# A gated linear-attention block with a SiLU-gated layer behind it: where the weights and activations begin in SBUF

## The chip, the cores and the metric

The kernel runs on one core of a Trainium2 chip. What counts is the device time of one execution in microseconds; the median of three runs is given. Each core has a matrix engine (PE in the profile, with its weight loads as PEld), a vector engine (DVE), a scalar engine (ACT), GpSimd (POOL), and a queue engine (SP) that starts the DMA transfers. SBUF is the on-chip memory of 128 partitions, PSUM the memory into which the matrix engine accumulates.

## What is computed

Per batch and head a complex 48 x 48 state is decayed step by step and read out by `q`; the result `x` (3072 tokens x 384) goes through a SiLU-gated layer. Cut to what matters:

```python
mag = np.sqrt(a_re * a_re + a_im * a_im)
scale = np.minimum(mag, 0.999) / (mag + 1e-06)
a_re_n, a_im_n = a_re * scale, a_im * scale
for t in range(S):                                   # S = 768, D = 48, 4 batches, 8 heads
    new_re = ar * S_re - ai * S_im
    new_im = ar * S_im + ai * S_re
    S_re, S_im = new_re + outer(k[t], v[t]), new_im
    y[t] = q[t] @ S_re
x = y.transpose(0, 2, 1, 3).reshape(3072, 384)
g = x @ w_gate                                       # 384 x 1536
out = (g / (1 + np.exp(-g)) * (x @ w_val)) @ w_out   # 1536 x 384
```

The weights arrive as 64-bit numbers; the kernel turns them into 32-bit ones on the chip.

## The kernel before

The tokens are cut into 24 slabs of 128 (6 chunks of time by 4 batches). Two slabs make a group, so there are 12 groups `g` of 256 tokens. The 1536 hidden columns of the gated layer are cut into 12 chunks `f` of 128. For each group the recurrence is turned into matmuls: `stage_ops` makes the decay factors on ACT and DVE, `slab_ops` the scores (line 630), the readout (line 661) and the state's update (line 667), and running sums over time are matmuls with a triangle of ones (line 457; line 454 in the first groups). The readout ends as `xh`, the group's activations rounded to the matrix engine's 32-bit fast format, and `xl`, the remainder.

`ffn_ops(g)` then runs over the 12 chunks. For each chunk, `f1` (line 847) makes gate and value: for each of the two, and for each of three slices of the 384 inputs, the products high weight x `xh`, high weight x `xl`, low weight x `xh`. That is 18 matmuls of 256 columns. In them a 128 x 128 block of weights is the stationary operand, and the activations are the moving operand, read as 256 consecutive 4-byte words of each partition. ACT applies SiLU (853), DVE multiplies with the value (858), and the product is split in the same way into `hh` and `hl` (lines 311, 313 and 307). `f2` (line 881) multiplies with `w_out`: two halves of 128 tokens by three products, 6 matmuls of 384 columns. Here the roles are turned: `hh` or `hl` is stationary, and the weights are moving, 384 consecutive words. Group 0 is exact: it uses the whole weights in single products in plain 32-bit, 6 in `f1` and 4 records per chunk in `f2`, reading every second word of the 64-bit storage.

The order of all instructions is made when the program is written, by a planner (`Planner.plan`) that holds an estimated cost for each step and hands out a fixed list. It knows costs, dependences, the number of buffers and due times (`key`), and nothing of addresses. The matrix engine works through its list in order; so does each other engine.

Where the operands lie. `place(nm, f, dtype)` (line 221) makes a tile of a chunk's weights: 1536 words of a partition for gate and value (`nm` "w"), 768 for `w_out` ("o"). The 64-bit words of chunk `f` are loaded into `place(nm, f)` by SP (line 737), put together on DVE (lines 746, 750, 754), and split into high and low halves (`c4`, `c5`) into the tile of the chunk before, `place(nm, f - 1)`. From then on chunk `f` is read from there: the high half at the tile's start, the low half 768 or 384 words behind it. Before the weights come, some of these tiles are lent to group 0's stages (`fixed`, line 268); after the split, the last chunk's tiles (`spare`, line 227) take the transfers for the range checks (line 795) and sector checks (818). `new(tag, inst)` (line 279) makes the other tiles. For the tags in `SHIFTED` (`xh`, `xl`, `hh`, `hl`) it makes the tile 64 words longer and begins 48 words, three times 64 bytes, behind its start.

Of the kernel before, what the change touches and what calls it, by code (L numbers as in the profile page):

```python
# [19 lines left out]
P = 128  # L20
# [172 lines left out]
def quick(ctx, tc, q, k, v, a_re, a_im, w_gate, w_val, w_out, out, count):  # L193
# [4 lines left out]
    work = ctx.enter_context(tc.tile_pool(name="work", bufs=1))  # L198
# [20 lines left out]
    WIDE = {"w": 2 * DM, "o": DM}  # L219

    def place(nm, f, dtype):

        return work.tile([P, 2 * WIDE[nm]], dtype, name=f"w{nm}{f}", tag=f"w{nm}{f}", bufs=1)

    tile_t = const.tile([P, 4 * DM], F32, name="turned")

    def spare(nm):

        if nm not in W:
            W.pop((nm, NF - 1, WHOLE))  # L230
            W[nm] = place(nm, NF - 1, F32)
        return W[nm]
# [21 lines left out]
    for t in STAGES:  # L254
        SHAPE[t] = ([P, 2 * H, D], F32)
    slots = dict(qs=1, ks=1, T=2, dec=3, sc=2, sg=2, hh=2, hl=2, ost=2, xh=2, xl=2, vt=2,
                 gv=2, po=1, ps=2, py=1, pm=1)
# [6 lines left out]
    for t, (nm, f, i) in {"re": ("w", 0, 0), "im": ("w", 0, 1), "s1": ("o", 0, 0), "s2": ("w", 1, 0), "s3": ("w", 1, 1),  # L264
                          "qt": ("o", 1, 0), "kt": ("o", 2, 0), "qs": ("w", 2, 0)}.items():
        n, nm_f = 96 if t == "qs" else D, (nm, NF - 3 + f)
        if nm_f not in W:
            W[nm_f] = place(*nm_f, F32)
        at = W[nm_f][:, i * A2:i * A2 + 2 * H * n].rearrange("p (h d) -> p h d", d=n)
        for j in range(2):  # L270
            fixed["lent", t, j] = at[:, H * j:H * j + H], nm_f
# [4 lines left out]
    pl = Planner(slots)  # L276
    at_ = {}

    def new(tag, inst):
        if tag in fixed:  # L280
            t = fixed[tag][0]
        elif tag[0] in ("ww", "wo", "bt"):
            t = None
        elif tag in PSUMS:
            t = psum.tile([P, 512], F32, name="p_" + tag, tag=tag, bufs=2 if tag == "po" else slots[tag])
        else:
            shape, dt = SHAPE[tag]
            if isinstance(inst, tuple) and inst[0] in SPLIT:
                dt = F32R
            if tag == "xh" and inst == 0:  # L290
                dt = F32
            if tag == "xl" and isinstance(inst, str):
                dt = U32
            if tag in SHIFTED:
                n = shape[-1] * (shape[1] if len(shape) > 2 else 1)
                t = work.tile([P, n + 64], dt, name=tag, tag=tag, bufs=slots[tag])[:, 48:48 + n]
                if len(shape) > 2:
                    t = t.rearrange("p (k t) -> p k t", k=KT)
            elif tag == "dec":
                t = work.tile([96, 8 * H], dt, name=tag, tag=tag, bufs=slots[tag])[:, 0:4 * H]  # L300
            else:
                t = work.tile(shape, dt, name=tag, tag=tag, bufs=slots[tag])
        at_[tag, inst] = t
        return t
# [26 lines left out]
    def stage_ops(g, first, many):  # L331
# [19 lines left out]
        def load(t, x):  # L351
            def fn(e):
                b0 = 2 * bp + first
                nc.sync.dma_start(out=new(*tg(t)).rearrange("p (b h) d -> p b (h d)", b=many), in_=x[b0:b0 + many, :, c * P:c * P + P, :].rearrange("b h t d -> t b (h d)"))
            pl.add(f"ld_{t}{N}", {"SP": 0.5}, fn, deps=[held.get(t, "")], alloc=[tg(t)], lat=1.4 if N == "0a" and t in ("re", "im") else LAND if exact else LAND + SPARE, move=0.65 * many)

        def act(name, dst, source, func, table, deps, scale=1.0, bias=None, new_=False):
            def fn(e):
                if new_:
                    new(*tg(dst))  # L360
                kw = {} if bias is None else {"bias": bias}
                nc.scalar.activation(out=of(dst), in_=of(source), func=func, scale=scale, **kw)  # L362
            length = cost(("ACT",), span)
            if bias is not None:
                length["ACT"] += 0.1
            pl.add(name + N, length, fn, deps=[d if "." in d else d + N for d in deps] + [held.get(name, "")], alloc=[tg(dst)] if new_ else [],
                   use=[tg(source)] + ([] if new_ else [tg(dst)]), table=table)
# [4 lines left out]
        if divided:  # L372
            def rec(e):
                nc.vector.reciprocal(out=new(*tg("s3")), in_=of("re"))
            pl.add("rec" + N, {"DVE": 2.5 * span / HD}, rec, deps=["ld_re" + N], alloc=[tg("s3")], use=[tg("re")])
        else:
            act("lnr", "s3", "re", AF.Ln, "ln", ["ld_re"], new_=True)
# [343 lines left out]
    def weight_ops(f):  # L721
        for nm, n, user in (("w", 2 * DM, "f1"), ("o", DM, "f2")):
# [5 lines left out]
            for i, w in enumerate((w_out,) if nm == "o" else (w_gate, w_val)):  # L728
                def ld(e, i=i, w=w, raw=raw, nm=nm):
                    if i == 0:  # L730
                        W.pop((nm, f), None)
                        W[nm, f, WHOLE] = place(nm, f, U32)
                        raw["all"] = W[nm, f, WHOLE].rearrange("p (n t) -> p n t", t=2)
                        raw["low"], raw["high"] = (raw["all"][:, :, x] for x in range(2))
                    o = raw["all"]
                    o = o if nm == "o" else o[:, i * DM:i * DM + DM].rearrange("p (k n) t -> p k n t", k=KT)
                    nc.sync.dma_start(out=o, in_=words(w, nm, f))
                loads.append(pl.add(f"wl{i}{N}", {"SP": 0.55}, ld, alloc=[] if i else lent, deps=list(loads), lat=LAND, move=1.09))
# [360 lines left out]
@with_exitstack  # L1099
def tile_kernel(ctx, tc, q, k, v, a_re, a_im, w_gate, w_val, w_out, out):  # L1100
    nc = tc.nc
    w_gate, w_val, w_out = (w if w.dtype == U32 else w.bitcast(U32) for w in (w_gate, w_val, w_out))
    keep = ctx.enter_context(tc.tile_pool(name="keep", bufs=1))

    count = keep.tile([1, 32], I32, name="count")[:, 0:1]
    quick(tc, q, k, v, a_re, a_im, w_gate, w_val, w_out, out, count)
    fit = nc.values_load(count, min_val=0, max_val=P)
    with tc.If(fit < P):
        general(tc, q, k, v, a_re, a_im, w_gate, w_val, w_out, out)
# [34 lines left out]
```

## Time and profile before

| what | value |
|---|---|
| median of 3 runs | 634.52 us (634.34 to 634.69) |
| the profiled execution's own time | 634.72 us |
| its span, first to last instruction | 632.9 us |
| PE busy | 615.9 us (97%) |
| DVE busy | 492.1 us (78%) |
| ACT busy | 427.0 us (67%) |
| POOL busy | 37.7 us (6%) |
| granted clock of PE, mean | 0.997 |
| moved by DMA | 80.66 MB, mean 127 GB/s |

The span leaves 1.8 us of the execution's time outside. Busy times of PE overlap and their ends are modelled, so a matmul's cost is read from the start of one to the start of the next, not from its duration. The chain of work that ended last says which engine sets the end; the timeline and the windows show the pace inside a stretch.

### The profile page before, as it was taken

Reading aid. Unit: us, or ns where it says so; the run is one execution under the profiler, and the core shown is the slowest. Engines: PE = TensorE matmul, PEld = TensorE weight load, DVE = VectorE, ACT = ScalarE, POOL = GpSimd, SP = SyncE. Lnnn points to the kernel's source line nnn. Section 1 sums busy time; section 2 is a strip of 40 time slices with the busy share of each in tenths; the row PEclk is TensorE's granted clock in tenths of the full one; section 3 lists DMA queues with packets and bytes.
Section 4 is the critical chain, followed back from the end, with each engine's and each line's share of the span. In section 5 each row is a group of like instructions: output and inputs, shape, how many; then the busy total and the mean of one; then the engine's idle time right before and its main releaser. Section 6 shows DMA issues by size and latency. Waiting matters only on the chain.

```text
span 632.9 us, 15752 instructions
## 1 busy us (share of the span) xinstructions
PE 615.9 (97%) x6380; PEld 590.9 (93%) x6380; DVE 492.1 (78%) x896; ACT 427.0 (67%) x693; POOL 37.7 (6%) x64
## 2 busy tenths in 40 slices
PE   8889999999999999999999999999999999999995
PEld 7677788899999999999999999999999999999995
DVE  6999999999978888779758779768769767543432
ACT  7973677987856976967967867977968973212210
POOL 1310001001010001001000010010000000000000
PEclk9999999999999999999999999999999999999998
DMA  9999213344463554464444464454443433421200
GB/s 284 324 337 305 38 50 94 74 111 123 121 149 108 147 135 117 122 150 116 129 123 119 122 163 110 118 152 127 127 125 104 139 85 94 122 74 51 76 1 30
DMA packets 133983, 80.66 MB, mean 127 GB/s; under 512 B 94320, under 2 KB 130160, under 8 KB 133904
## 3 DMA queue, kind: packets, MB, share of 16 engines
q1 hardware_dynamic: 131648, 75.52, 43.7%
q0 software_dynamic: 2256, 4.06, 2.9%
q8 instruction: 52, 0.85, 0.6%
q14 instruction: 27, 0.22, 0.1%
HBM read 59.04 MB, written 4.78 MB: 101 GB/s over the span
## 4 chain that ended last, share of the span: by engine, by line
PE 72%; DVE 3%; ACT 3%; issue 1%; ACTq 0%; DVEq 0%
PE p_gv L847 38%; PE p_po L881 20%; PE p_py L661 6%; PE p_ps L630 5%; PE p_pm L457 2%; PE p_pm L667 2%; ACT L971 1%; ACT s L362 1%; DVE wo L307 0%; DVE ww L307 0%; DVE sg L858 0%; DVE s L307 0%; DVE hl L307 0%; DVE sc L636 0%; ACT sg L853 0%
## 5 line engine op out<-in xcount | busy, mean ns | idle before, releaser
L847 PE MATMUL p_gv<-xh,ww 128*128 128x256 f32 x1596 | 310.1, 291 | 2.3 <-DVE sg L858 1.4
L847 PEld LDWEIGHTS p_gv<-xh,ww 128*128 128x128 f32 x1596 | 258.2, 190 | 9.1 <-DVE sg L858 3.2
L847 PE MATMUL p_gv<-xl,ww 128*128 128x256 f32 x726 | 203.0, 280 | 0.0
L971 ACT ACT_TABLE_LOAD x123 | 157.8, 1283 | 2.2
L847 PEld LDWEIGHTS p_gv<-xl,ww 128*128 128x128 f32 x726 | 136.4, 188 | 0.0
L853 ACT ACTIVATE sg<-p_gv 128x256 f32<-128x256 f32 x144 | 54.7, 383 | 106.6 <-PE p_gv L847 102.4
L881 PE MATMUL p_po<-wo,hh 128*128 128x384 f32 x484 | 126.4, 342 | 0.0
L858 DVE TENSOR_TENSOR sg<-sg,p_gv 128x256 f32<-128x256 f32 x144 | 59.0, 412 | 67.4 <-ACT sg L853 66.9
L881 PEld LDWEIGHTS p_po<-wo,hh 128*128 128x128 f32 x484 | 80.8, 188 | 1.1 <-issue 0.2
L881 PE MATMUL p_po<-wo,hl 128*128 128x384 f32 x242 | 81.5, 337 | 0.0
L307 DVE TENSOR_TENSOR hl<-sg,hh 128x256 fp32r<-128x256 f32 x132 | 55.0, 418 | 5.8 <-ACT hh L311 1.5
L630 PE MATMUL p_ps<-T 96*128 96x128 f32 x384 | 52.9, 279 | 0.0
L630 PEld LDWEIGHTS p_ps<-T 96*128 96x128 f32 x384 | 50.9, 196 | 0.6
L311 ACT CAST hh<-sg 128x256 fp32r<-128x256 f32 x68 | 27.5, 404 | 33.1 <-PE p_po L881 15.3
L881 PEld LDWEIGHTS p_po<-wo,hl 128*128 128x128 f32 x242 | 45.4, 188 | 0.0
L362 ACT ACTIVATE s<-s 128x768 f32<-128x768 f32 x44 | 37.2, 845 | 9.5 <-DVE s L307 7.6
L661 PE MATMUL p_py<-sc,vt 128*32 128x128 f32 x768 | 36.5, 272 | 1.1 <-ACT xh L685 1.1
L661 PE MATMUL p_py<-T,G 96*32 96x128 f32 x640 | 33.5, 280 | 0.0
L636 DVE TENSOR_TENSOR sc<-p_ps,tri 128x512 f32<-128x512 f32 x48 | 32.4, 678 | 0.5 <-PE p_ps L630 0.3
L847 PE MATMUL p_gv<-xh,ww-1_399 128*128 128x256 f32 x132 | 25.3, 283 | 0.0
L685 ACT CAST xh<-p_py 128x384 fp32r<-128x384 f32 x22 | 10.5, 478 | 21.6 <-PE p_py L661 21.4
L661 PEld LDWEIGHTS p_py<-sc,vt 128*32 128x32 f32 x768 | 22.8, 109 | 2.4 <-ACT xh L685 1.3
(140 smaller groups left out, 856.9 us busy)
## 6 DMA issues: line engine op xcount, KB each, us to landing
T<-turned SPq DMA_DIRECT2D x240, 64.0 KB, 2.1
wo<-in_moe_w_out_dram SPq DMA_DIRECT2D x24, 384.0 KB, 5.5
ww<-in_moe_w_gate_dram SPq DMA_DIRECT2D x12, 384.0 KB, 8.0
vt<-in_v_dram SPq DMA_DIRECT2D x24, 192.0 KB, 3.9
ww<-in_moe_w_val_dram SPq DMA_DIRECT2D x12, 384.0 KB, 8.6
out_dram<-ost SPq DMA_DIRECT2D x24, 192.0 KB, 2.0
wo<-in_moe_w_gate_dram SPq DMA_DIRECT2D x12, 384.0 KB, 3.6
wo<-in_moe_w_val_dram SPq DMA_DIRECT2D x12, 384.0 KB, 3.5
```

What stands on the lines that cost most here:

```text
L307: V[e].tensor_tensor(out=out, in0=a, in1=b, op=op)
L311: nc.scalar.copy(out=out, in_=in_)
L362: nc.scalar.activation(out=of(dst), in_=of(source), func=func, scale=scale, **kw)
L457: nc.tensor.matmul(out=ps, lhsT=tri, rhs=flat(half(x, i)), start=j == 0, stop=j == 1)
L630: nc.tensor.matmul(out=ps[:, hh, :], lhsT=kT(4 * qd + hh), rhs=qT(4 * qd + hh), start=True, stop=True)
L636: nc.vector.tensor_tensor(out=s, in0=at_["ps", f"{n}.{qd}"].rearrange("p (h t) -> p h t", h=4), in1=mask.unsqueeze(1).to_broadcast([P, 4, ...
L661: nc.tensor.matmul(out=o, lhsT=l, rhs=r, start=opens, stop=closes, tile_position=(0, 32 * slot))
L847: nc.tensor.matmul(out=gv[:, i, :], lhsT=l, rhs=r, start=(m == 0), stop=(m == len(mm) - 1))
L853: nc.scalar.activation(out=new("sg", I), in_=at_["gv", I][:, 0:2 * P], func=AF.Silu)
L858: nc.vector.tensor_tensor(out=sg, in0=sg, in1=at_["gv", I][:, 2 * P:4 * P], op=ALU.mult)
L881: nc.tensor.matmul(out=po, lhsT=l[:, cs], rhs=weight("o", f, part), start=f == 0 and j == 0, stop=f == NF - 1 and j == len(products) - 1)
L971: nc.scalar.preload_act_table_set(op.load)
```

## The change

Each tile of weights grows by 16 words (64 bytes). Its content begins `2 * ((f + 1) % 8)` words behind the tile's start, with `f` the number of the tile. Chunk `f` of the split weights lies in tile `f - 1`, so it begins `2 * (f % 8)` words, 0 to 56 bytes, behind a multiple of 64 bytes: chunks 0 and 8 at 0, chunks 1 and 9 at 2 words, and so on up to chunk 7 at 14 words. The loads of the raw words into tile `f` and the work lent to these tiles begin at that tile's offset too. For the tags of `SHIFTED` the content begins 48 words behind the tile's start in even groups, as before, and 50 words in odd groups. As a matmul's blocks are 128, 256 or 384 words apart, all operands of a chunk or group share its offset. No step is added, taken away or reordered. Tiles that are allocated behind a tile of weights move by whole multiples of 64 bytes.

```diff
     def place(nm, f, dtype):
 
-        return work.tile([P, 2 * WIDE[nm]], dtype, name=f"w{nm}{f}", tag=f"w{nm}{f}", bufs=1)
+        n, at = 2 * WIDE[nm], 2 * ((f + 1) % 8)
+        return work.tile([P, n + 16], dtype, name=f"w{nm}{f}", tag=f"w{nm}{f}", bufs=1)[:, at:at + n]
...
+    def tag_group(inst):
+
+        if isinstance(inst, int):
+            return inst
+        return int(inst.split(".")[0]) if "." in inst else 0
...
             if tag in SHIFTED:
                 n = shape[-1] * (shape[1] if len(shape) > 2 else 1)
-                t = work.tile([P, n + 64], dt, name=tag, tag=tag, bufs=slots[tag])[:, 48:48 + n]
+                begin = 48 + 2 * (tag_group(inst) % 2)
+                t = work.tile([P, n + 64], dt, name=tag, tag=tag, bufs=slots[tag])[:, begin:begin + n]
```

## Rows read from the trace of the kernel before

**Rows 1.** The page: busy time and share of each engine, and the chain that ended last by engine and by line.

```profile
PE 615.9 (97%) x6380; PEld 590.9 (93%) x6380; DVE 492.1 (78%) x896; ACT 427.0 (67%) x693; POOL 37.7 (6%) x64
...
PE 72%; DVE 3%; ACT 3%; issue 1%; ACTq 0%; DVEq 0%
```

**Rows 2.** Busy time of each engine in stretches of the span, with the granted clock of PE, the DMA engines' share and what they moved.

```profile
20.00:40.00 20.00, 16.11 (x248) 13.71 (x247) 19.85 (x34) 17.26 (x31) 6.16 (x9) 1.00 1.09 330
40.00:60.00 20.00, 18.27 (x91) 14.92 (x92) 20.00 (x36) 10.55 (x15) 0.00 (x0) 1.00 1.10 332
60.00:80.00 20.00, 20.00 (x157) 15.74 (x156) 20.00 (x35) 11.14 (x14) 1.36 (x2) 1.00 0.29 54
...
200.00:250.00 50.00, 50.00 (x563) 49.45 (x562) 43.30 (x72) 38.80 (x62) 3.09 (x5) 1.00 0.48 124
...
550.00:600.00 50.00, 50.00 (x479) 49.24 (x478) 21.15 (x52) 11.68 (x34) 0.00 (x0) 1.00 0.27 77
```

**Rows 3.** Groups of matmuls of lines 847 and 881, shapes apart: count, then busy time, mean duration of one, idle time before. The name `ww-1_399` is a tile of weights that the trace tells apart.

```profile
L847 PE MATMUL p_gv<-xh,ww 128*128 128x256 f32 x1596 | 310.1, 291 | 2.3 <-DVE sg L858 1.4 <-ACT T L311 0.7
L847 PE MATMUL p_gv<-xl,ww 128*128 128x256 f32 x726 | 203.0, 280 | 0.0
...
L881 PE MATMUL p_po<-wo,hh 128*128 128x384 f32 x484 | 126.4, 342 | 0.0
L881 PE MATMUL p_po<-wo,hl 128*128 128x384 f32 x242 | 81.5, 337 | 0.0
...
L881 PE MATMUL p_po<-wo-1_354,hh 128*128 128x384 f32 x44 | 11.5, 343 | 0.0
```

**Rows 4.** Timeline of PE around 303 us: the first two and the last record of an `f1` call of 18 matmuls, the first of the `f2` call behind it, and the first of the next `f1` call. Start, then length of the merged records.

```profile
302.00 0.28 PE L847 MATMUL p_gv<-xh,ww 128*128 128x256 f32 x1
302.11 0.28 PE L847 MATMUL p_gv<-xl,ww 128*128 128x256 f32 x1
...
304.00 0.28 PE L847 MATMUL p_gv<-xh,ww 128*128 128x256 f32 x1
304.12 0.52 PE L881 MATMUL p_po<-wo,hh 128*128 128x384 f32 x2
...
305.17 0.28 PE L847 MATMUL p_gv<-xh,ww 128*128 128x256 f32 x1
```

**Rows 5.** Timeline of PE around 181 us: the running sums ahead of another `f1` call, its first and last record, and the start of the `f2` call behind it.

```profile
180.18 0.34 PE L457 MATMUL p_pm<-re,tri 128*128 128x384 f32 x1
180.36 0.28 PE L847 MATMUL p_gv<-xh,ww 128*128 128x256 f32 x1
...
182.29 0.28 PE L847 MATMUL p_gv<-xh,ww 128*128 128x256 f32 x1
182.40 0.51 PE L881 MATMUL p_po<-wo,hh 128*128 128x384 f32 x2
```

**Rows 6.** The chain that ended last, in order of time, from 169 us on: start, length, line and count. The calls of 18 (`f1`) listed there are 75 of 2.12 us, 31 of 2.04 to 2.06 and 9 longer ones; those of 6 (`f2`) are 49 of 1.05 or 12 longer ones, and others of 1.04 below the list's limit. Shown are the first and the last calls and some between.

```profile
174.25 2.06 PE p_gv L847 x18
...
499.49 0.94 PE p_ps L630 x8
500.43 2.06 PE p_gv L847 x18
502.49 0.94 PE p_ps L630 x8
503.43 1.04 PE p_po L881 x6
...
553.70 2.12 PE p_gv L847 x18
555.81 1.05 PE p_po L881 x6
556.86 2.12 PE p_gv L847 x18
...
620.98 2.12 PE p_gv L847 x18
```

**Rows 7.** Two stretches of PE with a moving operand of 384 plain 32-bit words: group 0's `f2`, which reads every second word, and the running sums, which read consecutive ones (timeline); and the mean duration of one of each (groups by line, shapes apart).

```profile
47.41 1.52 PE L881 MATMUL p_po<-wo,sg 128*128 128x384 f32 x4
...
27.81 0.81 PE L454 MATMUL p_pm<-s,tri 128*128 128x384 f32 x2
...
L881 PE MATMUL p_po<-wo,sg 128*128 128x384 f32 x48 | 18.1, 502 | 0.0
...
L454 PE MATMUL p_pm<-s,tri 128*128 128x384 f32 x4 | 1.6, 487 | 0.0
```

**Rows 8.** Timeline of PE: the scores of four heads, two records each. By the code every second head's operands begin one word (4 bytes) behind the first one's, and every second word is read. Then the mean duration of such a record.

```profile
547.35 1.10 PE L630 MATMUL p_ps<-T 96*128 96x128 f32 x8
...
L630 PE MATMUL p_ps<-T 96*128 96x128 f32 x384 | 52.9, 279 | 0.0
```

**Rows 9.** DVE's steps on the raw weights: durations (shortest, median, longest) of the first step, whose input begins 4 bytes behind the tile's start and takes every second word, and the group of the third step with its mean.

```profile
L746 DVE TENSOR_SCALAR xl<-ww x12: 541/544/553, 28.7 to 84.0; 128x768 uint32<-128x768 uint32 x12
...
L754 DVE SCALAR_TENSOR_TENSOR ww<-ww,xl 128x768 uint32<-128x768 uint32 x12 | 11.3, 943 | 0.0
```

**Rows 10.** The weights' loads: time from issue to landing over all loads of line 737, the issue of chunk 0's last load on SP's queue, and the first DVE step that uses it.

```profile
DMA to landing us min/median/max: 6.3/8.4/10.0
...
17.66 0.37 SPq L737 DMA_DIRECT2D ww<-in_moe_w_val_dram  x1
...
28.67 0.55 DVE L746 TENSOR_SCALAR xl<-ww 128x768 uint32<-128x768 uint32 x1
```

## The prediction, made before the changed kernel was run

> **What bounds the kernel now.** I read the page's shares first: PE is busy 97% of the span, and 72% of the chain that ended last is PE, with DVE and ACT at 3% each [rows 1]. A share over the span can hide stages, so the windows come next. From 200 us on PE is busy 50 of 50 us in every stretch, and still at 550 us, where DVE has fallen to 21 and ACT to 12 us of 50 [rows 2]: there the end is set by the pace of the matmuls alone. Before that, from 20 to 80 us, DVE is full (19.85 of 20, then 20 of 20) and so, until 60 us, are the DMA engines (share 1.09 and 1.10); PE has holes there [rows 2]. So two stages are at stake: the start, set by DVE with the loads just ahead of it, and some 450 us of matmuls, nearly all of them lines 847 and 881 [rows 3]. The granted clock is 1.00 throughout, so PE runs at 2.4 GHz, and a word per cycle would be 106.7 ns for 256 columns.
>
> The timeline gives the pace there. One `f1` call runs from 302.00 to 304.12: 2.12/18 = 117.8 ns per matmul. The `f2` call behind it takes 1.05/6 = 175.0 ns [rows 4]. Another `f1` call, behind running sums, goes from 180.36 to 182.40: 113.3 ns [rows 5]. So the same shape at the same alignment has **two paces**. The chain shows which is common: 75 calls of 2.12 us, 31 of 2.04 to 2.06; the fast ones mostly follow scores or running sums, the slow ones an `f2` call [rows 6]. Both are above 106.7 ns. The fast one is 272 cycles for 256 words, 17 for each 16 words. 16 words are 64 bytes, so this looks like a price of 113.3/16 = **7.08 ns per 64 bytes** read, and 24 such pieces would make 170 ns for `f2`, which takes 175.0. The reading of every second word fits: with 384 plain 32-bit words it takes (1.52 - 0.50)/3 = 0.340 us per matmul, or 48 times 7.08 ns, where consecutive words take 0.81 - 0.49 = 0.32 us [rows 7]. There two cycles per word leave the fetch time, unless the words lie apart. What counts seems to be the span of memory that a moving operand covers, and whether the covered pieces are whole is what the change alters.
>
> **What the change does, part by part.** No instruction, wait or buffer is added, and the planner does not know addresses, so the order stays and nothing is queued behind anything new. Five things move by 8 to 56 bytes.
>
> 1. *`f1`'s moving operand, odd groups.* `xh` and `xl` begin 8 bytes behind a multiple of 64, so 1024 bytes touch 17 pieces in place of 16. That is 6 groups x 12 chunks x 18 = 1296 matmuls. No row shows such an operand; the bounds are the rows with more pieces. Above: a whole piece at the full rate, 7.08 ns. Below: in the slower stream of rows 7, 24 more pieces cost 20 ns, 0.8 ns each. Nothing is possible too, if pieces are counted from the operand's start, and less than nothing is the second rival.
>
> 2. *`f2`'s moving operand.* The weights begin off a multiple in all chunks but 0 and 8: 11 groups x 10 chunks x 6 = 660 matmuls with 25 pieces in place of 24, with the same bounds. (Group 0 has 40 more records; at 7.08 ns 0.3 us, left out.)
>
> If each of these 1956 paid 7.08 ns, it would be 13.8 us; at 0.8 ns 1.6 us. I take less than the upper end, because the slow pace has a pause in which another piece can be fetched. A slow `f1` matmul has 117.8 - 113.3 = 4.5 ns of it, `f2` 175.0 - 170.0 = 5.0 ns. A fast call pays in full. With 31 fast calls of 106, 21 of the 72 odd calls are fast and 51 slow. With pieces of 64 bytes that gives 21 x 18 x 7.08 = 2.7 us, 51 x 18 x 2.6 = 2.4 us, and 660 x 2.1 = 1.4 us: together 6.5 us. The rows fix the rate, not the size of a piece. With pieces of 32 bytes the extra one costs 3.54 ns, the pauses swallow it, and only the fast calls pay: 21 x 18 x 3.54 = 1.3 us. I know of no row that chooses, and take the middle, **3.9 us**.
>
> 3. *Stationary operands:* weights in `f1`, `hh` and `hl` in `f2`. They are loaded beside the running matmul, and 128 words, even 9 pieces of 7.08 ns, are 64 ns, well within 113.3. I put them at nothing; the cover is the matmul before.
> The Trainium skill, "TensorE: Matmul & The Clock Gate", section "Step-by-step: what each phase is for", says that PE has two independent SBUF read ports, so loading the next weights takes no read bandwidth from the running matmul. By that rule this part is exactly nothing; the two paces of one shape leave room for doubt, since no row explains them.
>
> 4. *DVE and ACT on these tiles.* The first step on the raw weights begins 4 bytes off a multiple and takes every second word, and still does 768 words in 0.544 us where a two-input step takes 0.943 [rows 9]. So a start off a multiple doesn't cost DVE its fast form. Nothing; if it did, the 12 steps would add 12 x 0.4 = 4.8 us to a full DVE.
>
> 5. *Loads into the tiles.* Chunk 0's last load is issued at 17.66; with the median of 8.4 us it lands at 26.1, and DVE's first step on it runs at 28.67 [rows 10]. A lead of 2.6 us covers small losses. Later loads run further ahead: the DMA share falls to 0.29 after 60 us, with DVE still full [rows 2]. Nothing, with the third rival if not.
>
> Attention's own tiles move by multiples of 64 bytes; the scores go at (1.10 - 0.28)/7 = 0.117 us a record with heads on and 4 bytes off a multiple [rows 8], so I expect nothing there. One pause of 4.5 ns more or less on 384 records would be 1.7 us either way.
>
> **The sum:** 634.72 (the profiled execution, span 632.9 and 1.8 around it) + 3.9 = 638.6; the median of the runs is 0.2 us lower, so I say **638.5 us**. With the ends of the unknown price this case runs from 634.5 + 1.3 = 635.8 to 634.5 + 13.8 = 648.3.
>
> **The rivals.**
>
> *The offset costs nothing (634.5, within 1.2 us).* For it: the heads that begin 4 bytes off go as fast as the others [rows 8], though with every second of 256 words they cover no more pieces. Or the pieces are small enough for all to fit into the pauses.
> The Trainium skill, "SBUF — State Buffer", section "Specifications (TRN2)", speaks of lines of 16 bytes and of a penalty for each crossing to a new one. By that an operand 8 bytes off touches one more small line, a quarter of 7.08 ns, or some 0.7 us over the fast odd calls: an estimate that falls in this rival, and no run here shows it.
>
> *Faster: the slow pace goes.* The two paces at one alignment mean that something between the load of weights and the moving stream can fall in step or not. The weights' offset, different in each chunk, shifts one against the other by 2 to 14 words. If that keeps them out of step, a slow call of 2.12 becomes one of 2.05 us: 0.07 us for each of the 75, scaled to 132 calls 6.5 us, and `f2` at 170.0 in place of 175.0 another 132 x 0.03 = 4.0 us. All of it would give 624; the more probable half, in the groups whose activations stay aligned and some others, 629. It decides as soon as the calls turned outnumber the extra pieces: at 3.9 us of these, 56 calls. Against it: a call keeps its pace through 18 matmuls, whichever it has, so the state holds itself.
>
> *The start gets longer.* If loads to odd addresses land later by as much as the slowest here against the median, 10.0 to 8.4, or 19% [rows 10], then 40 us at full share become 7.6 us longer; less the lead of 2.6 that is 5.0: 639.5 without any change of pace.
> The Trainium skill, "DMA: Bandwidth & Descriptors", section "How a descriptor splits into AXI transactions", lets a transaction start only at a multiple of 256 bytes, so that a piece that begins off one needs a transaction more. By it a run of 1024 bytes could take 5 in place of 4; on the loads' 40 us, if the SBUF side set their rate, an estimate of 10 us. No row shows whether it does.
>
> *The change does not do what it says* has little room: tiles still start at multiples of 64 bytes by the code, and the offset is a plain slice.
>
> **How the numbers follow.** Extra pieces 0.50, nothing 0.24, slow pace gone 0.21, longer start 0.05. The range must leave out no more than 2 in 10. Below 630 lies about half of the faster case, 0.10; above 645 the upper end of the pieces' case, 0.09: 630.0 to 645.0. A measurement here can tell about 0.2%, 1.3 us. Faster takes 0.21. Slower takes the pieces' case but for a little that falls under 1.3 us, and the longer start: 0.53. The same is 0.26.
>
> **What would show it.** Right: the `f1` calls of odd groups rise from 2.12 and 2.05 toward 2.17, those of even groups stay; `f2` goes from 1.05 to some 1.06 or 1.07 except in chunks 0 and 8; the part up to 100 us keeps its length. Wrong: odd and even groups alike; calls that differ by chunk within an even group (then the stationary offset counts); more calls at 2.05 than before; or a first `f1` call of group 1 that starts later.

## The result and the profile after

The changed kernel takes **640.83 us** (median of 4 runs, 640.59 to 641.45) against 634.45 us (4 runs, 634.34 to 634.69): ratio 1.010, 95% interval 1.0088 to 1.0112. It is 6.4 us slower. The forecast was 638.5 us within 630 to 645: the sign was right, the size too small by 2.3 us. The profiled execution after has a span of 639.7 us against 632.9, with the same instructions in the same order.

The page of after, busy shares and the chain by engine (they answer to [rows 1]):

```profile
PE 622.7 (97%) x6380; PEld 598.2 (94%) x6380; DVE 493.1 (77%) x896; ACT 427.5 (67%) x693; POOL 37.5 (6%) x64
...
PE 85%; ACT 8%; DVE 3%; issue 2%; DMA 1%; SPq 0%; DVEq 0%; ACTq 0%
```

PE's busy time has grown by 6.8 us, which is the whole of the span's growth; DVE's and ACT's by 1.0 and 0.5. Where it came in shows in the windows, the stretches of [rows 2]:

```profile
20.00:40.00 20.00, 16.03 (x248) 13.63 (x246) 19.89 (x34) 17.24 (x32) 6.04 (x9) 1.00 1.09 336
40.00:60.00 20.00, 18.33 (x91) 14.91 (x92) 20.00 (x36) 10.48 (x15) 0.00 (x0) 1.00 1.08 336
60.00:80.00 20.00, 20.00 (x157) 15.82 (x156) 20.00 (x35) 11.14 (x14) 1.36 (x2) 1.00 0.31 60
200.00:250.00 50.00, 50.00 (x559) 49.59 (x558) 42.55 (x71) 38.78 (x60) 3.08 (x5) 1.00 0.47 121
550.00:600.00 50.00, 50.00 (x478) 49.22 (x477) 23.19 (x52) 12.09 (x35) 0.00 (x0) 1.00 0.26 72
```

Up to 80 us the rows are those of before to within 0.2 us, and the clock is 1.00 as before. From 200 us on PE is as full as before but gets through fewer matmuls, 559 for 563 and 478 for 479: the pace. The timeline puts the first `f1` record of group 1 at the same place in both: the first line below is from before, the second and all that follow from after.

```profile
102.89 0.59 PE L847 MATMUL p_gv<-xh,ww-1_399 128*128 128x256 f32 x1
102.87 0.59 PE L855 MATMUL p_gv<-xh,ww-1_399 128*128 128x256 f32 x1
...
582.50 0.28 PE L855 MATMUL p_gv<-xh,ww 128*128 128x256 f32 x1
...
584.60 0.53 PE L889 MATMUL p_po<-wo,hh 128*128 128x384 f32 x2
...
614.63 0.28 PE L855 MATMUL p_gv<-xh,ww 128*128 128x256 f32 x1
...
616.82 0.51 PE L889 MATMUL p_po<-wo,hh 128*128 128x384 f32 x2
...
617.87 0.29 PE L855 MATMUL p_gv<-xh,ww 128*128 128x256 f32 x1
```

Line 847 is 855 here, 881 is 889; in the experiments these numbers shift with each edit, and the tiles `p_gv` (`f1`) and `p_po` (`f2`) tell which call is meant. "Call" stands for the 18 matmuls of `f1`, or the 6 of `f2`, of one chunk. The call at 582.50 is one of an even group (group 10): 2.10/18 = 117 ns per matmul. The call at 614.63 is one of an odd group (11): 2.19/18 = 121.7 ns; the `f2` call behind it takes 1.05. The chain that ended last, in order of time, shows the step from group 10 to 11 at 592 us (start, length, count; compare [rows 6]):

```profile
579.49 2.12 PE p_gv L855 x18
581.60 1.06 PE p_po L889 x6
582.66 2.11 PE p_gv L855 x18
...
589.02 2.13 PE p_gv L855 x18
591.15 1.05 PE p_po L889 x6
592.20 2.16 PE p_gv L855 x18
...
595.40 2.17 PE p_gv L855 x18
...
627.67 2.18 PE p_gv L855 x18
```

Of the calls of 18 that this list has, 31 took 2.04 to 2.06 before and 75 took 2.12 [rows 6]; after, **none is below 2.10**, and the largest groups are 2.16 (19), 2.17 (19) and 2.18 (18). So two things happened: odd groups slowed to some 2.17, and the calls at 2.05 are gone, in even groups too.

One table for all kernels, worked out from the start of every matmul in each trace. `f1` is the mean interval from one start to the next inside a call (intervals over 130 ns, in which another step came between, are left out; a call without such an interval is called undisturbed below); "fast" counts, of the 132 calls of groups 1 to 11, those whose median interval is at most 114 ns; `f2` is the median over the calls. The last column is the ratio with its interval where the kernel was timed, else the time of one run beside one run of before. That run, 633.84 us, lies at the low end of all runs of before (633.83 to 635.36), so the time differences of the single runs with it are uncertain by about 1 us, and their paces say more.

| kernel | f1 odd / even, ns | fast odd / even | f2 odd / even, ns | time |
|---|---|---|---|---|
| before | 116.3 / 116.6 | 25 / 16 | 174.6 / 174.4 | 634.45 us |
| after | 120.6 / 118.2 | 0 / 0 | 176.7 / 176.0 | 1.010 (1.0088 to 1.0112) |
| e1_acts | 120.3 / 116.2 | 0 / 24 | 177.0 / 174.6 | 1.0063 (1.0049 to 1.0076) |
| e2_weights | 118.1 / 118.2 | 0 / 0 | 176.5 / 175.9 | 1.0069 (1.0055 to 1.0083) |
| e3_pad | 118.2 / 118.3 | 0 / 0 | 175.8 / 175.8 | 1.0061 (1.0048 to 1.0075) |
| e12_four | 117.7 / 116.4 | 0 / 21 | 176.0 / 174.4 | 1.0027 (1.0018 to 1.0037) |
| e10_hodd | 116.6 / 116.7 | 23 / 16 | 175.8 / 174.4 | 1.0009 (1.0000 to 1.0019) |
| e11_padfix | 117.0 / 117.2 | 15 / 11 | 176.0 / 175.6 | 1.0026 (1.0015 to 1.0036) |
| e9_h16 | 116.2 / 116.1 | 31 / 27 | 173.6 / 173.6 | 0.9994 (0.9985 to 1.0003) |
| e6_wsub | 117.6 / 117.6 | 13 / 12 | 174.4 / 174.4 | 635.99, before 633.84 us |
| e8_osub | 116.3 / 116.2 | 26 / 24 | 175.8 / 175.8 | 635.04, before 633.84 us |
| e7_hlines | 115.7 / 115.9 | 38 / 27 | 174.4 / 175.7 | 633.52, before 633.84 us |

The two tables by group and offset follow with e4 and e5. The sum of after: 72 odd calls x 17 intervals x 4.3 ns = 5.3 us, 60 even ones x 17 x 1.6 ns = 1.6 us; summed from the records themselves, from first to last start in each call, it is 5.1 and 1.6, and 1.05 for `f2`. That is 7.7 us of the span's 6.8: the rest of the span takes 0.9 less, and where is not known. One trace stands for each kernel, and the groups that an experiment left alone moved by up to 0.4 us in these sums.

### The profile page after: what moved, and what is told of

It reads as the page before. It is cut to its first block, busy times and chain, and to the rows that moved or that the text cites. A ratio compares the mean times of both kernels' runs of the same rounds, so it can differ in the third digit from the quotient of the medians.

```text
span 639.7 us, 15752 instructions
## 1 busy us (share of the span) xinstructions
PE 622.7 (97%) x6380; PEld 598.2 (94%) x6380; DVE 493.1 (77%) x896; ACT 427.5 (67%) x693; POOL 37.5 (6%) x64
## 4 chain that ended last, share of the span: by engine, by line
PE 85%; ACT 8%; DVE 3%; issue 2%; DMA 1%; SPq 0%; DVEq 0%; ACTq 0%
PE p_gv L855 45%; PE p_po L889 23%; PE p_py L669 6%; PE p_ps L638 6%; ACT L979 3%; PE p_pm L465 2%; PE p_pm L675 2%; ACT s L370 1%; DMA ww<-in_a_im_dram 1%; DVE ks L315 1%; PE p_gv L590 1%; DVE xl L758 0%; ACT sg L861 0%; DVE ww L315 0%; DVE sc L644 0%
## 5 line engine op out<-in xcount | busy, mean ns | idle before, releaser
L855 PE MATMUL p_gv<-xh,ww 128*128 128x256 f32 x1596 | 316.6, 293 | 1.6 <-DVE sg L866 0.8
L315 DVE TENSOR_TENSOR s<-im,s 128x768 fp32r<-128x768 f32 x10 | 9.6, 956 | 20.3 <-PE p_pm L465 20.3
```

The costliest lines, as they stand in the source:

```text
L315: V[e].tensor_tensor(out=out, in0=a, in1=b, op=op)
L855: nc.tensor.matmul(out=gv[:, i, :], lhsT=l, rhs=r, start=(m == 0), stop=(m == len(mm) - 1))
```

## The experiments

The theory to start from is the prediction's, A: a moving operand off a multiple of 64 bytes touches one more piece and pays for it. The trace of after spoke against it as the whole cause, since even groups, whose activations stayed on multiples of 64 bytes, slowed too. Rivals: B, a stationary operand off a multiple costs as well; C, the moves of all other tiles by whole steps of 64 bytes did it; D, what counts is the distance between weights and activations in whole steps of 64 bytes, which the change alters because every tile of weights grew by 64 bytes.

### Each half alone, and the growth alone

e1_acts has only the part of the change that moves the activations:

```diff
-                t = work.tile([P, n + 64], ...)[:, 48:48 + n]
+                begin = 48 + 2 * (tag_group(inst) % 2)
+                t = work.tile([P, n + 64], ...)[:, begin:begin + n]
```

> Only the odd groups' activations (xh, xl, hh, hl) begin 2 words off; the weights lie as before. Theory A (a moving operand that begins off a multiple of 64 bytes touches one more piece, at 7.08 ns): f1 of odd groups goes at 17 pieces, 120.4 ns, in all chunks; even groups keep their two paces of 113.3 and 117.6; f2 as before. In time 6 groups x 12 x 18 x (120.4 - 116.4) = 5.2 us: 639.6. Theory B (what counts is how far weights and activations lie apart within 64 bytes, in f1 and f2 alike): as they are now 2 words apart in odd groups, f1 and f2 of the odd groups both rise, f2 to 176: some 0.6 us more, 640.2, and the paces need not be 120.4. Theory C (the other tiles' moves by 64 bytes did it): 634.5.

Measured: 638.43 us (5 runs, 638.09 to 638.82), 4.0 more than before. Only odd groups pay. The chain, from group 10 to 11 (from 589.37 on):

```profile
586.20 2.12 PE p_gv L854 x18
588.32 1.05 PE p_po L888 x6
589.37 2.16 PE p_gv L854 x18
591.53 1.05 PE p_po L888 x6
592.58 2.16 PE p_gv L854 x18
594.74 1.05 PE p_po L888 x6
595.79 2.17 PE p_gv L854 x18
```

The undisturbed odd calls run at a median of 120.1 or 120.2 ns in every chunk (50 of the 56 at 120.1 to 120.3, the rest at up to 121.0), and no odd call is fast any more. That is close to A's number, 17/16 of 113.3, or 120.4. But `f2` rose too in odd groups, 174.6 to 177.0, where of its own operands only the stationary ones had moved.

e2_weights has only the part that makes the tiles of weights:

```diff
-        return work.tile([P, 2 * WIDE[nm]], ...)
+        n, at = 2 * WIDE[nm], 2 * ((f + 1) % 8)
+        return work.tile([P, n + 16], ...)[:, at:at + n]
```

> Only the weights begin 0 to 14 words off; all activations lie as before. Theory A: f1 has aligned moving operands in all groups and stays as before, f2 goes toward 25 pieces, 177, in all chunks but 0 and 8; 1 us more, 635.5. Theory B: f1 loses its fast pace in all groups, as the even groups of the changed kernel did (1.56 us over 5 groups, so 3.4 over 11), and f2 gives 1 us: 638.9. Theory C: as with the change, 640.

Measured: 638.79 us (5 runs, 638.22 to 639.25), 4.4 more. `f1` costs 3.7 us of it, although its moving operands stayed on multiples of 64 bytes: no call is fast, in odd or in even groups.

e3_pad keeps the growth of the tiles and takes the offset away:

```diff
-        return work.tile([P, 2 * WIDE[nm]], ...)
+        n, at = 2 * WIDE[nm], 0
+        return work.tile([P, n + 16], ...)[:, at:at + n]
```

> The weights' tiles grow by 16 words, and nothing begins off a multiple of 64 bytes: only the other tiles and the weights move by multiples of 64. Theories A and B: 634.5, with both paces of f1 as before. Theory C: up to 641. If the number of 64-byte steps between weights and activations counts, f1's pace differs by chunk, as each chunk's tile is moved by another number of steps.

Measured: 638.13 us (5 runs, 637.9 to 638.75), **3.7 more, with every operand on a multiple of 64 bytes**. `f1` reads 118.2 and 118.3 ns, as in e2_weights, and again no call is fast. A and B had 634.5 us here, so neither is the whole cause. The intervals of e2 and e3 overlap, so the weights' offsets proper add nothing that can be told on top of the growth. This was the surprise of the case: the 64 bytes that were only to make room cost nearly as much as all that was meant to be tried.

### What the offset costs in itself

e4_table leaves the weights alone and gives `xh` and `xl` another offset in each group:

```diff
+                begin = 48 + (0, 0, 1, 2, 4, 6, 8, 10, 12, 14, 15, 0)[tag_group(inst)] * (tag in ("xh", "xl"))
```

> Weights as before; xh and xl of groups 1 to 11 begin 0, 1, 2, 4, 6, 8, 10, 12, 14, 15, 0 words behind a multiple of 64 bytes, to read f1's pace by group. Theory A with pieces of 64 bytes: 120.4 ns in groups 2 to 10, whatever the offset, and the old two paces in 1 and 11; about 640. With pieces of 32 bytes: group 6 (8 words) like the aligned ones, the others 116.8. With pieces of 16 bytes: groups 4, 6 and 8 (4, 8, 12 words) like the aligned ones. Theory B: a pace that depends on the offset, best somewhere between 2 and 14.

Measured (one run): 638.58 us, against 634.40 for the median of before. The pace of most undisturbed calls of each group:

| words off | 0 | 1 | 2 | 4 | 6 | 8 | 10 | 12 | 14 | 15 |
|---|---|---|---|---|---|---|---|---|---|---|
| f1, ns | 117.5, some 113.4 | 119.8 | 120.1 | 116.8, some 119.1 | 121.6, some 119.6 to 120.8 | 118.2 | 120.5 | 116.8 to 117.5 | 119.7 | 117.8 |

Two groups in the chain of this kernel, 4 words off (at 257) and 6 words off (at 300):

```profile
257.49 2.10 PE p_gv L854 x18
259.60 1.04 PE p_po L888 x6
...
300.15 2.19 PE p_gv L854 x18
302.33 1.04 PE p_po L888 x6
```

2.10/18 is 116.8 ns and 2.19/18 is 121.6. With pieces of 64 bytes every offset but 0 should cost the same. Instead the multiples of 4 words, 16 bytes, mostly stay at 116.8 to 118.2 (three calls at 4 words take 119.1), and of the others all but 15 words pay some 3 ns more. So e12_four repeats e1_acts with 4 words in place of 2:

```diff
+                begin = 48 + 4 * (tag_group(inst) % 2)
```

> As the run with the activations alone (2 words off in odd groups, 638.4 us, f1 120.1 to 120.3 ns there), but 4 words off, that is 16 bytes. If a moving operand is read in pieces of 64 bytes, as the prediction's step 1 has it, 4 words touch a seventeenth piece as 2 words do: f1 120.4 ns in odd groups, 638.4 us. If the pieces have 16 bytes, 256 words from there touch 64 of them as before: f1 116.8 to 117.8 ns as in the group of the table that stood 4 words off, the call pace of 113.3 lost in odd groups (at most a third of 72 calls x 18 x 4 ns = 1.7 us) or replaced by 116.8: 633.8 to 636.

Measured: 636.02 us (10 runs; before 634.39), ratio 1.0027 against 1.0063 for 2 words, with intervals that do not touch; it is at the upper end of what pieces of 16 bytes were to give, 636. The chain at the same step from group 10 to 11 (from 587.49 on):

```profile
584.33 2.12 PE p_gv L854 x18
586.45 1.05 PE p_po L888 x6
587.49 2.10 PE p_gv L854 x18
589.60 1.04 PE p_po L888 x6
590.64 2.10 PE p_gv L854 x18
```

Odd calls take 2.10 there where e1_acts has 2.16 to 2.17: of the 55 undisturbed ones 42 run at 116.8 ns, the other 13 at 118.8 to 119.1. **What matters of a moving operand's start is whether it lies on a multiple of 16 bytes, not of 64**, and the prediction's piece of 64 fell here. This is not the whole of it: no odd call is at 113.3 any more, and neither the second pace of 119 ns nor 15 words in the table is explained. The 1.6 us that remain lie in the 25 fast calls that odd groups lost, in the calls at 119, and in `f2`, which is at 176.0 there.

### Stationary operands

e10_hodd moves `hh` and `hl` alone, 2 words in odd groups:

```diff
+                begin = 48 + 2 * (tag_group(inst) % 2) * (tag in ("hh", "hl"))
```

> Only hh and hl move, by 2 words, in odd groups: the stationary operands of f2, streamed by nothing. If a stationary operand off a 64-byte multiple costs as well: f2 in odd groups 176 to 177 ns against 174.4, even groups unchanged, some 0.6 us, 634.7 to 635.5. Rival, the prediction's step 3, a stationary operand costs nothing behind the running matmul, and f2's rise in the run with all four activations moved came from xh and xl: f2 174.4 in both, 634.4.

Measured: 635.11 us (10 runs; before 634.58), ratio 1.0009. `f2` in odd groups 175.8 against 174.6, even ones unchanged at 174.4. The step is B's, a little below the 176 to 177 expected; in time it is 0.5 us and lies at the edge of what can be told. It is half of the 2.4 ns of e1_acts; `f2` also goes by what is done to `xh` and `xl`, for it falls to 173.0 in most groups of e4_table, where they alone moved. So the 176.0 of e12_four, in which all four tiles stand 4 words off, belongs beside the 177.0 of e1_acts, and what 4 words cost `hh` and `hl` alone is not tested.

e6_wsub moves the weights of gate and value, stationary in `f1`, by 2 to 14 words in chunks 1 to 7, with tiles padded by 256 bytes, so that nothing else changes its place modulo 256:

```diff
+        at, pad = (2 * (f + 1), 64) if nm == "w" and 0 <= f <= 6 else (0, 0)
+        return work.tile([P, n + pad], ...)[:, at:at + n]
```

> Gate and value weights of chunks 1 to 7 begin 2, 4, 6, 8, 10, 12, 14 words off, all else at multiples of 64 and at the old distances of 64-byte steps (the tiles grow by 256 bytes, a whole number of the kernel's 256-byte grid). Theory A (stationary operands cost nothing): f1 of chunks 1 to 7 keeps both old paces, 634.4. Theory B (the distance within 64 bytes counts too): chunks 1 to 7 lose the pace of 113.3 and go at 116 to 119, by chunk; about +1.5 us. Chunks 0 and 8 to 11 as before in both.

Measured (one run): 635.99 us, 2.2 more than the single run of before; the `f1` calls of its trace take 2.5 us more in all. In the chain of group 11, chunk 1 (590.48), 3 (596.82), 5 (603.12) and 8 (612.71):

```profile
590.48 2.12 PE p_gv L849 x18
...
596.82 2.08 PE p_gv L849 x18
...
603.12 2.16 PE p_gv L849 x18
...
612.71 2.12 PE p_gv L849 x18
```

Chunks 1 to 7 run at 118.1, 118.5, 115.2, 118.5, 119.8, 120.0 and 119.3 ns; the others keep both old paces. Only 9 calls of the seven chunks are fast, all of chunk 3 (6 words), where 30 were before; the other chunks have 16, where 11 were. So B holds in `f1` too, and not as a plain price: the chunk 6 words off is quicker than the slow pace at 0. Nor do multiples of 16 bytes help a stationary operand: 4, 8 and 12 words off give 118.5, 118.5 and 120.0.

e8_osub does the same to the output weights, which move in `f2` (the edit is that of e6_wsub with `nm == "o"`).

> As the run before, but for the output weights (moving in f2): chunks 1 to 7 begin 2 to 14 words off. Theory A with pieces of 16 bytes (as the table of activations suggests): f2 of chunks 2, 4 and 6 (4, 8, 12 words) stays near 174, chunks 1, 3, 5, 7 rise by 2 to 4 ns; f1 unchanged; less than 1 us. With pieces of 64 bytes all seven rise alike.

Measured (one run): 635.04 us, 1.2 more, where less than 1 was expected. `f2` by words off: 2: 178.4, 4: 173.6, 6: 177.3, 8: 176.8, 10: 176.4, 12: 175.0, 14: 180.2, and 173.6 to 174.6 in the chunks left in place. Again 4 words cost nothing and 12 little, and the offsets between multiples of 4 cost 2 to 6 ns; 8 words, at 2 ns, do not fit.

### Whole steps of 64 bytes

By the program's allocation all tiles of weights lie 128 bytes behind a multiple of 256 before, and `xh` and `xl` begin 64 behind one: one step of 64 below the weights. e5_lines moves `xh` and `xl` to 0, 16, 32 and 48 words by group, all multiples of 64 bytes:

```diff
+                begin = 16 * (tag_group(inst) % 4) if tag in ("xh", "xl") else 48
```

> Weights and all other tiles as before; only xh and xl begin 0, 16, 32 or 48 words behind their tiles' start in groups with g mod 4 = 0, 1, 2, 3 (before: 48 in all), so that the distance from weights to activations takes four values in steps of 64 bytes and nothing lies off a multiple of 64. Theory D (the distance in 64-byte steps sets the pace, and the pace of 113.3 ns exists at some distances only): groups 3, 7 and 11 keep 113.3 and 117.5; at least the two even distances (16 and 48 differ from them) go at 116.5 to 120 with no call at 113.3, as with the grown tiles; about +2 us. Theory E (the other tiles' moves did it): all groups as before, 634.4.

Measured (one run): 637.18 us, 3.3 more. Chain, groups 8 (0 words), 10 (32 words) and 11 (48 words, as before):

```profile
445.82 2.16 PE p_gv L854 x18
...
582.33 2.13 PE p_gv L854 x18
...
591.86 2.12 PE p_gv L854 x18
```

| begin of `xh`, `xl`, words | 0 | 16 | 32 | 48 (before) |
|---|---|---|---|---|
| f1, ns | 119.4 to 120.2 | 117.8 | 118.6 | 117.5 and 113.3 |

The fast pace is there at one distance of four, and a distance can cost as much as a bad offset. e11_padfix then keeps the grown tiles of e3_pad and moves `xh` and `xl` back to one step below a multiple of 256:

```diff
+                begin = {"xh": 64, "xl": 32}.get(tag, 48)
```

> The weights' tiles 16 words longer and nothing off a 64-byte multiple, as in the run that cost 3.7 us, but xh begins 64 and xl 32 words behind its tile's start, so that both lie one 64-byte step below a multiple of 256 bytes. By the tiles' addresses the weights of chunks 1, 4, 6, 8 and 11 then lie one step above xh and xl modulo 256, as all chunks do before; those of 0 and 2 two steps and of 3, 5, 7, 9, 10 three. If the distance between weights and activations sets f1's pace: 113.3 ns comes back in some calls of chunks 1, 4, 6, 8 and 11 and in no other chunk; 636 to 637.5. Rival, the growth of the tiles costs by itself (the grid of 256 bytes, whatever the activations do): no call at 113.3, 638.1 as there.

Measured: 636.22 us (8 runs; before 634.58), ratio 1.0026 against 1.0061 for e3_pad, with intervals that do not touch. The same call in the timelines of both, group 4, chunk 6: first and last record, and the first of the `f2` call behind it. First e3_pad, 2.15/18 = 119.4 ns:

```profile
274.47 0.28 PE L848 MATMUL p_gv<-xh,ww 128*128 128x256 f32 x1
...
276.51 0.28 PE L848 MATMUL p_gv<-xh,ww 128*128 128x256 f32 x1
276.62 0.51 PE L882 MATMUL p_po<-wo,hh 128*128 128x384 f32 x2
```

Then e11_padfix, 2.04/18 = 113.3:

```profile
274.12 0.28 PE L855 MATMUL p_gv<-xh,ww 128*128 128x256 f32 x1
...
276.05 0.28 PE L855 MATMUL p_gv<-xh,ww 128*128 128x256 f32 x1
276.16 0.51 PE L889 MATMUL p_po<-wo,hh 128*128 128x384 f32 x2
```

All 13 undisturbed calls below 115 ns are in chunks 1, 4, 6, 8 and 11, the five that were named beforehand. Counted by the median interval, 26 calls have the 113.3-ns pace: 19 of the 55 calls of these chunks and 7 of the 77 of the others, all 7 with another step in between, where none was expected. So the rule is strong but not clean. Chunks at another distance show 117.8 (three steps) and 118.4 to 118.6 (two), close to e5_lines' 117.8 and 118.6. So distance is a part of what the growth cost, and setting it back regained 2.1 of the 3.7 us. That it is the whole is not shown: the edit also brought `xh` and `xl`, which the growth had set apart, to the same place modulo 256. And distance from `xh` alone is not the rule: by the program's allocation `xh` lies no step from the weights of chunks 3, 5, 7, 9 and 10 in e3_pad, with `xl` two steps away, and these run at 116.5 to 118.2 ns, where e5_lines with both at no step has 119.4 to 120.2.

### Is there a better place for `hh` and `hl`?

```diff
+                begin = 16 * (tag_group(inst) % 4) if tag in ("hh", "hl") else 48    # e7_hlines
+                begin = 16 if tag in ("hh", "hl") else 48                            # e9_h16
```

> As before, but hh and hl (the stationary operand of f2) begin 0, 16, 32 or 48 words behind their tiles' start in groups with g mod 4 = 0, 1, 2, 3. Theory D: f2 goes at 173 to 178 ns by distance, 174.5 at 48 words; f1 unchanged but for what the pace of f2 does to it; within 0.7 us of 634.4. Theory E: f2 the same in all groups.

Measured (one run): 633.52 us, 0.3 less than before. `f2` by groups: 0 words 175.0, 16 words 172.2 to 173.6, 32 words 176.0, 48 words 174.5; and `f1`, whose operands had not moved, had 65 fast calls against 41. The gain is in the groups at 0 and 16 words, 40 of 60 calls where before had 21; the other groups have 25 of 72 where before had 20. Hence e9:

> Only hh and hl move, to 16 words behind their tiles' start in all groups (48 before). If the distance in 64-byte steps between an operand that is loaded and one that streams sets the pace, as the groups at 16 words showed in the run where hh and hl stood at 0, 16, 32 and 48 words by group: f2 at 172.2 to 173.6 ns per matmul in all groups against 174.4 before (132 calls x 6 x 1 to 2 ns = 0.8 to 1.6 us), and many more f1 calls at 113.3 ns (132 x 18 x 2.6 ns, the drop of those groups' median from 117.5 to 114.9, is up to 6 us): 628 to 632.5. Rival, those groups were fast by their place in the order and not by the address: 633.8 to 634.6, f2 at 174.4.

Measured: 634.0 us (11 runs; before 634.58, 25 runs), ratio 0.9994, interval 0.9985 to 1.0003: a miss. `f2` did come to 173.6 everywhere, but `f1` had 58 fast calls, not most of them, and the calls of both lines took 1.0 us less in all, not the several us that were expected. So the address of the operands of `f2` is at most a part of what sets the pace of `f1`.

Nor is a call's pace always fixed as it begins, as the prediction took it to be. It was so in 131 of the 132 calls of before, but 13 of the 58 fast calls here start at the slow pace and turn fast after five matmuls; in no trace does a call that starts fast turn slow. One such call, group 10, chunk 8 (a record x2 is two matmuls):

```profile
572.45 0.28 PE L854 MATMUL p_gv<-xh,ww 128*128 128x256 f32 x1
...
573.04 0.39 PE L854 MATMUL p_gv<-xh,ww 128*128 128x256 f32 x2
573.27 0.28 PE L854 MATMUL p_gv<-xl,ww 128*128 128x256 f32 x1
...
574.52 0.50 PE L888 MATMUL p_po<-wo,hh 128*128 128x384 f32 x2
```

The first five matmuls take (573.04 - 572.45)/5 = 118 ns each, the last eleven (574.52 - 573.27)/11 = 113.6.

## Why the prediction was right, and where its steps were wrong

*What bounds the kernel* held: the end moved by what the matmuls' pace cost. *Steps 4 and 5 and the third rival:* the start did not move. Group 1's first `f1` record is at 102.87 us after and 102.89 before; DVE's first step on the raw weights has a median of 552 ns against 544 [rows 9], and the loads land in 8.2 us against 8.4 [rows 10]:

```profile
L754 DVE TENSOR_SCALAR xl<-ww x12: 545/552/557, 28.6 to 84.0; 128x768 uint32<-128x768 uint32 x12
...
DMA to landing us min/median/max: 5.7/8.2/9.9
```

The Trainium skill, "DMA: Bandwidth & Descriptors", section "How a descriptor splits into AXI transactions", has a run such as these of 1024 bytes, where it starts off a multiple of 256 bytes, take one transaction more. The prediction's estimate from it overlooked where the tiles lay: by the program's allocation they began 128 bytes behind such a multiple before, so by this rule a run takes five transactions before and, in all tiles but one, after. The landing times do not test the rule.

*Step 1, `f1` in odd groups*, named the right place and effect, and its upper sum the right size. With an extra piece at the full rate it had 2.7 us from the calls at 113.3 ns and 2.4 from those at 117.8, 5.1 together; measured are 5.1 with the growth in it, and 4.6 in e1_acts without. In e1_acts both kinds of call end at 120.2 ns, 6.9 above 113.3 and 2.7 above 117.5, as the step's 7.08 and 2.6 had it. **The step that failed is the choice of the middle**: the sum with pieces of 32 bytes, 1.3 us, was given as much weight as the one of 6.5, and 3.9 came out (added up, 638.4 rather than 638.5). The reason behind the upper sum failed too, since multiples of 16 bytes decide (e4_table, e12_four): 4 words off should have cost as much as 2, and does not. So the 7.08 ns are the size of what was seen, and not the price of a fetch of 64 bytes. That the whole sum of 6.5 us is so near the 6.4 measured is partly chance, as the even groups' 1.6 us were not in it.

The Trainium skill, "SBUF — State Buffer", section "Specifications (TRN2)", has lines of 16 bytes and a penalty for crossing. For the moving operands the runs agree on the 16 bytes (e12_four, 1.0027 against 1.0063). The estimate drawn from it, a quarter of 7.08 ns for an extra line, was too small: 2 words off cost 4.0 ns a matmul over the odd groups of e1_acts.

*Step 2, `f2`*, is right in size: 1.05 us, where the two sums had 1.4 and nothing. The cause is mixed: offset weights alone gave 0.9 us (e8_osub), the growth alone 0.9 (e3_pad), offset stationary operands 0.4 (e10_hodd). They do not add up; that what one has slowed the other finds slow already would explain it, but is not shown for `f2`. The sign "except in chunks 0 and 8" came only in part: in even groups chunk 8 kept 173.4 ns, but chunk 0 went to 177.2, and the growth alone has it at 176.0 (e3_pad).

*Step 3, stationary operands at nothing, was wrong.* They cost in `f1` (e6_wsub, 2.2 us for seven chunks) and a little in `f2` (e10_hodd). The cover was argued from time, 64 ns of loading within 113.3. The traces do not have this 64: a record of a load takes some 190 ns, before (first line, mean behind the busy time) and after alike, and the loads overlap each other:

```profile
L847 PEld LDWEIGHTS p_gv<-xh,ww 128*128 128x128 f32 x1596 | 258.2, 190 | 9.1 <-DVE sg L858 3.2
L855 PEld LDWEIGHTS p_gv<-xh,ww 128*128 128x128 f32 x1596 | 260.1, 190 | 8.1 <-DVE sg L866 2.3
```

The Trainium skill, "TensorE: Matmul & The Clock Gate", section "Step-by-step: what each phase is for", with its two independent read ports, has no cost for this; e6_wsub differs from the "exactly nothing" that was drawn from it, and the measurement decides. How the place of the loaded operand comes to cost time is open. That loads and streams meet at the same part of the memory, by address modulo 256, would fit, but is argued, not shown.

*The step that was missing* is the growth of the tiles. The text said of attention's tiles that they move by multiples of 64 bytes and put that at nothing; it did not ask what the same move does to weights against activations. Alone it costs 3.7 us (e3_pad), and e11_padfix gave a good half of that back without touching the tiles. In after, the even groups' 1.6 us are the growth's (e3_pad has the same 1.6 there). In odd groups the 2 words alone cost 4.6 and the growth alone 2.2; together they cost 5.1. That is less than the two added, as a call can lose the fast pace only once.

*The rivals.* "Costs nothing" is out. "The slow pace goes" had the two paces right as the thing to watch, and the sign wrong: of 41 fast calls none was left. Of the signs named in advance, "calls that differ by chunk within an even group" came: 116.8 to 119.2 ns in group 4's undisturbed calls at its start, by chunk. But it does not show what it was to show, that the stationary offset counts: with the growth alone the chunks differ as much (117.4 to 119.6 in the same calls of e3_pad). What shows that is e6_wsub.

What stays open: what makes a call run at 113.3 rather than 117.5 ns with the same operands at the same places. The operands' addresses decide whether it can; e9_h16 shows that they do not decide whether it does. The step just ahead goes with it: before, 19 of 21 calls behind scores are fast, 10 of 21 behind running sums, and 9 of 81 behind an `f2` call. Why is not known.

## What to carry to other kernels

Where PE sets the end, where operands begin is part of the kernel: keep a moving operand's start on 16 bytes, and look at stationary and moving operands as a pair, modulo 256. Growing a tile to make room is itself a change: test the room alone before you test what goes into it. And in a trace, count the calls at each pace; a mean hides that one of two paces is gone.

## What was not expected of the hardware

- One shape at one clock, 128 x 128 by 256 columns, ran undisturbed at paces from 113.4 to 121.6 ns within one trace (e4_table), where only start addresses of its operands differ; two of these paces, 113.4 and 117.5, occur at the same addresses.
- With all operands on multiples of 64 bytes, four distances from weights to activations gave 119.4 to 120.2, 117.8, 118.6 and 117.5 or 113.3 ns (e5_lines).
- With a moving operand 4 words off most calls run at 116.8 ns, below the 117.5 of the aligned slow pace, others at some 119, and none at 113.3 (e4_table, e12_four).
- With `f1`'s operands left in place, moving `hh` and `hl`, which only `f2` reads, went with more fast `f1` calls: 65 (e7_hlines) and 58 (e9_h16) against 41, one trace each; in time e9_h16 cannot be told from before.
- A call can turn from the slow to the fast pace after five of its 18 matmuls (13 calls in e9_h16); in no trace did one turn from fast to slow.
